# An attention stage re-ordered: feature maps stationary in kv, slot logits from transposed x, three engines in source order

## The chip, the cores and the metric

One core of a Trainium2 chip runs the whole program. The metric is the device time of one execution in microseconds. The core has five engines with a queue each: TensorE (matmuls, PE in the profile), VectorE (DVE), ScalarE (ACT), GpSimd (POOL) and SyncE (SP), which here issues the transfers. PEld is TensorE loading its stationary operand.

## What is computed

Linear attention over 4 batches, 8 heads, 576 positions and 64 channels with 128 features, followed by two mixtures of experts. The change touches the attention and the slot logits of the first mixture.

```python
def phi(x):
    proj = einsum('bhsd,df->bhsf', x, w_phi)
    proj = proj - max(abs(proj), axis=-1)
    return concatenate([exp(proj), exp(-proj)], axis=-1)
q_p, k_p = phi(q), phi(k)
kv = einsum('bhsf,bhsd->bhfd', k_p, v)
z = sum(k_p, axis=2)
num = einsum('bhsf,bhfd->bhsd', q_p, kv)
den = einsum('bhsf,bhf->bhs', q_p, z) + 1e-06
x = num / den                       # then (2304, 512), heads side by side
logits = x @ moe_phi                # (2304, 32), first mixture
d = softmax(logits, axis=0); c = softmax(logits, axis=1)
slot_input = d.T @ x                # 32 slots, 8 experts, then c @ slot_out
...                                 # second mixture: 8 experts over all tokens
```

## The kernel before

The 2304 tokens are cut into 18 tiles of 128 tokens (NT = 18), all batches in one row. A batch has 4.5 tiles, so tiles 4 and 13 hold two batches, and there are 20 (tile, batch) blocks of v, whose rows of the other batch are zero. All of the attention runs in one loop over i from 0 to 25. The key side works at tile i, the query side at t = i - LAG with LAG = 7, so that iterations 0 to 6 have keys alone, 7 to 17 keys and queries, 18 to 25 queries alone.

- `project` (pk for keys, pq for queries) multiplies a tile of 512 x 128 by the feature matrix into two PSUM banks (heads of even and odd number), and VectorE then takes the largest magnitude per head (mk, mq) and subtracts it (uk, uq). uq and uk have two buffers each, one for each half of a tile.
- `k_exp` makes phik = exp(u), exp(-u) with four ScalarE instructions.
- `kv_acc` accumulates kv transposed, v as the stationary operand and 256 feature columns moving, for a (tile, batch) block. `z_acc` adds phik into zs elementwise on GpSimd, in the key-only part half of it on VectorE.
- `kv_finish`, once per batch, sums zs over partitions with ones (zp), turns kv back through a matrix bd which holds the identity and, beside it, the slot matrix phi (kvp), spreads z (zc), and leaves kvs with XW = 64 + 32 + 1 columns per head: values, slot logits, denominator.
- `q_transpose` turns uq (ut) and takes both exponentials (phiq). `q_num` multiplies phiq by kvs (num), adds 1e-6 to the denominator column, inverts it (rd), scales the 32 logit columns (lgh), sums them over heads (lg), and scales the values (x).
- `slot_inputs` is a generator per group of four tiles (the fifth group has two): column maximum (gm, gmt, mx, dg, gmb), exponential (dd), sums (pcs) and slot inputs (psi), with a running rescaling. `si_step` runs its next part, once in the middle and once at the end of an iteration. `slot_norm` makes the row softmax. `keep_busy` issues transposes that nobody reads.

The kernel uses PSUM as eight banks of 512 columns: the kv accumulator takes two, and a pool of six rotates among all other tiles (`mm`). Up to the end of the loop a planner orders the instructions of each engine; a wrapper `InOrder` makes an engine keep the source's order, and it is put on all five only behind the loop. The weights of the first mixture are 32 units of 1 MB. Their first buffers are free from the start, some become free with the key buffers (`wk`), and four (`wq`) with the query buffers after the loop. Lines written behind the loop stand in the profile under one helper line, L50.

Of the kernel before, what the change touches and what calls it, by code (L numbers as in the profile page):

```python
# [22 lines left out]
XW = D + NS + 1  # L23
# [30 lines left out]
def tile_kernel(ctx: ExitStack, tc: tile.TileContext, a):  # L54
# [84 lines left out]
    zs_t = {}  # L139
# [13 lines left out]
    def kv_acc(t, b):  # L153
        phik = phik_t[t]
        v = vt_t.pop(VBLOCKS.index((t, b)))
        first = b * S // 128 == t
        last = ((b + 1) * S - 1) // 128 == t
        if first:
            kvacc[b] = pacc.tile([128, 1024], F32, tag="kv", name=f"kvacc{b}")
        acc = kvacc[b]  # L160
        for p in range(4):
            for j in range(2):
                PE.matmul(  # L163
                    acc[64 * j:64 * j + 64, p * 256:(p + 1) * 256],
                    v[:, (2 * p + j) * D:(2 * p + j + 1) * D],
                    phik[:, 2 * p + j].rearrange("p c f -> p (c f)"),
                    start=first and p % 2 == 0, stop=last, skip_group_check=True,
                )

    def z_acc(t, b):  # L170
        flat = phik_t[t].rearrange("p h c f -> p (h c f)")
        _, r0, r1 = next(x for x in parts_of(t) if x[0] == b)
        if b not in zs_t:
            z = zs_t[b] = kp.tile([128, 2048], F32, tag="zs", name=f"zs{b}", bufs=1)
            if r0:
                G.memset(z[0:r0], 0.0)
            A.copy(out=z[r0:r1], in_=flat[r0:r1])
        else:
            z = zs_t[b]
            cut = 1024 if t < LAG else 2048  # L180
            G.tensor_tensor(out=z[r0:r1, 0:cut], in0=z[r0:r1, 0:cut], in1=flat[r0:r1, 0:cut], op=ALU.add)  # L181
            if cut < 2048:
                V.tensor_tensor(out=z[r0:r1, cut:], in0=z[r0:r1, cut:], in1=flat[r0:r1, cut:], op=ALU.add)

    def kv_finish(b):

        acc = kvacc.pop(b)
        kvt = kp.tile([128, 1024], F32, tag="kvt", name=f"kvt{b}", bufs=1)
        for i in range(2):
            A.copy(out=kvt[:, i * 512:(i + 1) * 512], in_=acc[:, i * 512:(i + 1) * 512])  # L190
        yield
        zs = zs_t.pop(b)
        zp = mm(f"zp{b}")
        for g in range(4):
            PE.matmul(zp[32 * g:32 * g + 32, :], ones[:, 0:32], zs[:, g * 512:(g + 1) * 512], start=True, stop=True)
        zrow = kp.tile([128, 512], F32, tag="zrow", name=f"zrow{b}", bufs=1)
        V.tensor_copy(out=zrow, in_=zp)
        kvs = qp.tile([128, 2, H, XW], F32, tag=f"kvs{b % 2}", name=f"kvs{b}", bufs=1)
        for c in range(2):
            pss = [mm(f"kvp{b}_{c}_{j}") for j in range(2)]  # L200
            for p in range(4):
                for j in range(2):
                    r = slice(j * D, (j + 1) * D)
                    for g in range(2):
                        f = p * 256 + c * 128 + g * 64
                        PE.matmul(
                            pss[j][g * 64:(g + 1) * 64, p * 96:(p + 1) * 96],
                            kvt[r, f:f + 64], bd[r, p, j * 96:(j + 1) * 96], start=True, stop=True,
                        )
            for j in range(2):  # L210
                (A.copy if j == 0 else V.tensor_copy)(
                    out=kvs[:, c, j::2, 0:XW - 1], in_=pss[j][:, 0:384].rearrange("p (h w) -> p h w", h=4),
                )
        zc = mm(f"zc{b}")
        for j in range(2):
            for c in range(2):
                o = (j * 2 + c) * 4
                for g in range(2):
                    f = j * 256 + c * 128 + g * 64
                    PE.matmul(zc[g * 64:(g + 1) * 64, o:o + 4], zrow[:, f:f + 64], sel_e, start=True, stop=True)  # L220

        for c in range(2):
            V.tensor_copy(
                out=kvs[:, c, :, XW - 1].rearrange("p (g j) -> p j g", j=2),
                in_=zc[:, 0:16].rearrange("p (j c g) -> p j c g", j=2, c=2)[:, :, c, :],
            )
        kvs_t[b] = kvs
        yield
# [19 lines left out]
    x_t, lgh_t = {}, {}  # L248

    def q_num(t, hh):  # L250
# [3 lines left out]
        if hh == 0:  # L254
            lgh_t[t] = qp.tile([128, H, NS], F32, tag="lgh", name=f"lgh{t}", bufs=1)
# [770 lines left out]
```

## Time and profile before

| | |
|---|---|
| median of three runs | 1042.41 us (1038.42 to 1042.95) |
| the profiled execution | 1041.55 us, span 1039.4 us |
| granted TensorE clock, mean | 0.993 of full |
| TensorE busy | 1011.1 us, 97% of the span |
| VectorE, ScalarE, GpSimd busy | 723.7, 549.4, 642.0 us |
| attention, to the last numerators | 0 to 198.7 us |
| first expert matmul of the first mixture | 206.41 us |

The span runs from the first to the last instruction; the execution's own time has about 2 us around it. A busy TensorE need not be at its peak, since its matmuls are pipelined: a group's length in the timeline includes the time in which its last matmul drains, and the distance from one group's start to the next says what it costs. From 300 us on the second mixture fills TensorE.

### The profile page before, as it was taken

Reading aid. Unit: us, or ns where it says so; the run is one execution under the profiler, and the core shown is the slowest. Engines: PE = TensorE matmul, PEld = TensorE weight load, DVE = VectorE, ACT = ScalarE, POOL = GpSimd, SP = SyncE. Lnnn points to the kernel's source line nnn. Section 1 sums busy time; section 2 is a strip of 40 time slices with the busy share of each in tenths; the row PEclk is TensorE's granted clock in tenths of the full one; section 3 lists DMA queues with packets and bytes.
Section 4 is the critical chain, followed back from the end, with each engine's and each line's share of the span. In section 5 each row is a group of like instructions: output and inputs, shape, how many; then the busy total and the mean of one; then the engine's idle time right before and its main releaser. Section 6 shows DMA issues by size and latency. Waiting matters only on the chain.

```text
span 1039.4 us, 25962 instructions
## 1 busy us (share of the span) xinstructions
PE 1011.1 (97%) x10673; PEld 934.9 (90%) x10673; DVE 723.7 (70%) x1498; ACT 549.4 (53%) x965; POOL 642.0 (62%) x408
## 2 busy tenths in 40 slices
PE   7998988998999999999999999999999999999998
PEld 4676767745999999999999999999999999999998
DVE  7888778723688676766766766676676766766765
ACT  5664433224566766665556555555655565556442
POOL 3543510047477858785787778677858785787543
PEclk9998989999999999999999999999999999999999
DMA  8962226398000310040013003100310040000111
GB/s 301 373 210 64 61 76 252 139 417 330 29 1 1 123 42 2 1 163 2 1 42 123 2 1 109 55 2 2 122 43 1 2 163 1 2 2 21 62 42 61
DMA packets 22581, 89.43 MB, mean 86 GB/s; under 512 B 2752, under 2 KB 5568, under 8 KB 14272
## 3 DMA queue, kind: packets, MB, share of 16 engines
q1 hardware_dynamic: 22176, 87.26, 23.1%
q8 instruction: 84, 1.38, 0.5%
q0 software_dynamic: 288, 0.52, 0.2%
q14 instruction: 33, 0.27, 0.1%
HBM read 83.05 MB, written 4.72 MB: 84 GB/s over the span
## 4 chain that ended last, share of the span: by engine, by line
PE 89%; DVE 6%; DMA 2%; issue 1%; POOL 1%; ACT 0%; SPq 0%; DVEq 0%; ACTq 0%; POOLq 0%
PE x L50 38%; PE y L50 19%; PE z L50 16%; PE num L262 4%; PE kvacc L163 2%; PE ut L236 2%; DMA moe_w<-in_moe_w 2%; PE pq L125 1%; PE ps L50 1%; DVE mq L132 1%; PE pk L125 1%; PE ph L50 1%; DVE uq L134 1%; PE po L50 1%; PE pr L50 1%
## 5 line engine op out<-in xcount | busy, mean ns | idle before, releaser
L50 POOL TENSOR_TENSOR hl_s<-s,hh_s 128x512 fp32r<-128x512 f32 x287 | 366.5, 1298 | 213.2 <-ACT hh_s L50 194.0
L50 PE MATMUL x<-w_t,hh_s 128*128 128x256 f32 x1152 | 204.3, 277 | 0.0
L50 ACT ACTIVATE hh_s<-s 128x512 fp32r<-128x512 f32 x288 | 175.5, 629 | 52.2 <-DVE s L50 47.9
L50 ACT ACTIVATE r<-z 128x512 f32<-128x512 f32 x144 | 86.2, 598 | 166.5 <-PE z L50 166.5
L50 PEld LDWEIGHTS x<-w_t,hh_s 128*128 128x128 f32 x1152 | 173.6, 188 | 0.0
L50 DVE SCALAR_TENSOR_TENSOR xo<-x,P,xo 128x256 f32<-128x256 f32 x252 | 120.8, 480 | 71.5 <-PE x L50 71.5
L50 ACT ACTIVATE hh_a<-z 128x512 fp32r<-128x512 f32 x216 | 122.2, 600 | 76.2 <-DVE s L50 75.3
L50 DVE SCALAR_TENSOR_TENSOR s<-z,r 128x512 f32<-128x512 f32 x144 | 98.8, 686 | 87.7 <-ACT hh_a L50 82.6
L50 PE MATMUL x<-w_t,hl_s 128*128 128x256 f32 x576 | 159.5, 277 | 0.0
L50 DVE SCALAR_TENSOR_TENSOR hl_a<-z,hh_a 128x512 fp32r<-128x512 f32 x216 | 147.1, 681 | 0.0
L50 PEld LDWEIGHTS x<-w_t,hl_s 128*128 128x128 f32 x576 | 108.3, 188 | 0.0
L50 PE MATMUL y<-w_t,hh_s 128*128 128x256 f32 x576 | 102.9, 278 | 0.0
L50 PE MATMUL z<-w_b,hh_a 128*128 128x256 f32 x576 | 102.3, 278 | 0.0
L50 PE MATMUL x<-w_t,hh_a 128*128 128x256 f32 x576 | 101.6, 276 | 0.0
L50 PE MATMUL y<-w_b,hh_s 128*128 128x256 f32 x576 | 101.5, 276 | 0.0
L50 PE MATMUL x<-w_b,hh_a 128*128 128x256 f32 x576 | 101.2, 276 | 0.1
L50 DVE SCALAR_TENSOR_TENSOR s<-z,s 128x512 f32<-128x512 f32 x144 | 98.4, 684 | 4.0 <-POOL hl_s L50 1.7
L181 POOL TENSOR_TENSOR zs<-zs,phik 128x2048 f32<-128x2048 f32 (+3 forms) x16 | 60.6, 3786 | 58.0 <-ACT phik L150 55.2
L50 PEld LDWEIGHTS z<-w_b,hh_a 128*128 128x128 f32 x576 | 86.6, 188 | 2.9 <-issue 2.9
L50 PEld LDWEIGHTS y<-w_t,hh_s 128*128 128x128 f32 x576 | 87.4, 188 | 0.0
L50 PEld LDWEIGHTS x<-w_b,hh_a 128*128 128x128 f32 x576 | 86.5, 188 | 0.4 <-ACT hh_a L50 0.4
L50 PEld LDWEIGHTS y<-w_b,hh_s 128*128 128x128 f32 x576 | 86.7, 188 | 0.0
(199 smaller groups left out, 2106.3 us busy)
## 6 DMA issues: line engine op xcount, KB each, us to landing
moe_w<-in_moe_w SPq DMA_DIRECT2D x64, 1024.0 KB, 7.6
vt<-in_vb SPq DMA_DIRECT2D x20, 256.0 KB, 3.8
kt<-in_kT SPq DMA_DIRECT2D x18, 256.0 KB, 5.7
qt<-in_qT SPq DMA_DIRECT2D x18, 256.0 KB, 3.5
out<-xo SPq DMA_DIRECT2D x18, 128.0 KB, 1.7
out<-xo SPq DMA_DIRECT2D x9, 256.0 KB, 2.0
rep<-in_rep POOLq DMA_DIRECT2D x2, 256.0 KB, 9.8
bd<-in_bd SPq DMA_DIRECT2D x1, 384.0 KB, 4.7
```

Source lines behind the costliest of these rows:

```text
L50: return lambda *args, **kwargs: self.tc.keep_in_program_order(make(*args, **kwargs))
L125: PE.matmul(pss[j][g * 64:(g + 1) * 64, p * F:(p + 1) * F], x[r, p * 128 + g * 64:p * 128 + (g + 1) * 64], wbd[r, j * F:(j + 1) * F], star ...
L132: V.tensor_reduce(out=m, in_=h4(pss[j]), axis=AX.X, op=ALU.max, apply_absolute_value=True)
L134: V.tensor_tensor(out=h4(u), in0=h4(pss[j]), in1=m.unsqueeze(2).to_broadcast([128, 4, F]), op=ALU.subtract)
L163: PE.matmul(acc[64 * j:64 * j + 64, p * 256:(p + 1) * 256], v[:, (2 * p + j) * D:(2 * p + j + 1) * D], phik[:, 2 * p + j].rearrange("p c f ...
L181: G.tensor_tensor(out=z[r0:r1, 0:cut], in0=z[r0:r1, 0:cut], in1=flat[r0:r1, 0:cut], op=ALU.add)
L236: PE.transpose(ps[:, j * 128:(j + 1) * 128], uq_t[t][hh][:, j * 128:(j + 1) * 128], ident)
L262: PE.matmul(ps[g * 64:(g + 1) * 64, j * XW:(j + 1) * XW], phiq[:, c, j * 128 + g * 64:j * 128 + (g + 1) * 64], kvs_t[b][:, c, 2 * j + hh, ...
```

## The change

- kv: phik becomes the stationary operand (two halves of 64 features), and v moves, 65 columns per head: a column of ones beside the 64 values makes z in the same matmul. The accumulator takes three banks. z_acc and the matmuls of kv_finish go; three ScalarE copies per batch make kvs, with XW = 65.
- v's tiles are loaded with 65 columns per head, so that each row lands in eight pieces of 256 bytes; GpSimd sets the ones. Six buffers instead of three, each load one iteration earlier.
- Slot logits: x is turned by TensorE (x_turn), copied by ScalarE, and multiplied by phi (x_logits), whose result ScalarE copies into lg. lgh and its sum over heads go.
- PSUM: five banks A to E, each tile's named by hand; the rotation remains for tiles behind the loop.
- TensorE, VectorE and ScalarE keep source order from ahead of the loop. In an iteration with keys the order is now: x_turn(t-1), query projection(t+1), key projection(i+1), both transposes(t), kv block, k_exp, x_logits(t-1), slot step, both numerators(t), a second kv block. Without keys x_turn follows the transposes and x_logits the numerators. The numerators of t come one iteration earlier than before.
- Weights: wa is loaded in iterations 5 to 8 (was 1 to 4), the next seven in 9 to 15 (was 5 to 11); sel4 and wg within the loop. slot_norm is cut in two parts, with its two wide operations on GpSimd for the first three groups; gm4's copy goes to GpSimd.

```diff
-XW = D + NS + 1
+XW = D + 1
+KVB = 6
...
+    def mm(name, bank=None):
+        if bank is None:
+            bank = "ABCDE"[turn_of[0] % 5]
+            turn_of[0] += 1
+        return pmm.tile([128, 512], F32, tag=bank, name=name)
...
+        x = kp.tile([128, H, XW], F32, tag="vt", name=f"vt{i}", bufs=6)
+        SP.dma_start(out=x[:, :, 0:D], in_=a["vb"][i].rearrange("p (h d) -> p h d", h=H))
...
+            G.memset(x[r0:r1, :, D:XW], float(b1 == b))
...
-        pss, us = [mm(f"p{nm}{t}_{j}") for j in range(2)], []
+        pss, us = [mm(f"p{nm}{t}_{j}", ("CD" if nm == "k" else "AB")[j]) for j in range(2)], []
...
+        for m in range(2 * H):
+            j, p, c = m // 8, m // 2 % 4, m % 2
+            h = 2 * p + j
+            o = m // KVB * 512 + m % KVB * XW
+            for g in range(2):
                 PE.matmul(
+                    acc[g * 64:(g + 1) * 64, o:o + XW],
+                    phik[:, h, c, g * 64:(g + 1) * 64], v[:, h, :],
+                    start=first and m % KVB == 0, stop=last, skip_group_check=True,
                 )
...
+        for i in range(3):
+            n = min(KVB, 2 * H - KVB * i) * XW
+            A.copy(out=kvs[:, i * KVB * XW:i * KVB * XW + n], in_=acc[:, i * 512:i * 512 + n])
...
+    def late(t):
+        return "C" if t + LAG + 1 >= NT else "A"
...
-        ps = mm(f"ut{t}_{hh}")
+        ps = mm(f"ut{t}_{hh}", "E" if hh == 0 else late(t))
...
-        ps = mm(f"num{t}_{hh}")
+        ps = mm(f"num{t}_{hh}", "E" if hh == 0 else late(t))
...
+    def x_turn(t):
+        ps = mm(f"xt{t}", "D" if t + LAG + 2 >= NT else "E")
+        for kc in range(KC):
+            PE.transpose(ps[:, kc * 128:(kc + 1) * 128], x_t[t][:, kc * 128:(kc + 1) * 128], ident)
+        xT = qp.tile([128, KC, 128], F32, tag="xT", name=f"xT{t}", bufs=1)
+        A.copy(out=xT.rearrange("p c t -> p (c t)"), in_=ps)
...
+    def x_logits(t):
+        xT = xT_t.pop(t)
+        pl = mm(f"lg{t}", "B")
+        for kc in range(KC):
+            for g in range(2):
+                PE.matmul(pl[g * 64:(g + 1) * 64, 0:NS], xT[:, kc, g * 64:(g + 1) * 64], phi[:, kc, :], start=kc == 0, stop=kc == KC - 1)
+        A.copy(out=lg[:, t, :], in_=pl[:, 0:NS])
...
-        pt = mm(f"gmt{g}")
-        keep_busy(last, 13)
+        pt = mm(f"gmt{g}", "C")
+        keep_busy(last, 5)
...
-        ps, pc = mm(f"psi{g}"), mm(f"pcs{g}")
+        ps, pc = mm(f"psi{g}", "B"), mm(f"pcs{g}", "C")
...
+        W = G if g < 3 else V
...
+    PE, V, A = (InOrder(tc, x) for x in (PE, V, A))
     k_project(0)
     k_exp(0)
     for i in range(NT + LAG + 1):
         t = i - LAG
+        alone = i + 1 >= NT
...
+        if 0 <= t - 1 < NT and not alone:
+            x_turn(t - 1)
+        if 0 <= t + 1 < NT:
+            q_project(t + 1)
         if i + 1 < NT:
             k_project(i + 1)
         if 0 <= t < NT:
             q_transpose(t, 0)
+            q_transpose(t, 1)
+        if 0 <= t - 1 < NT and alone:
+            x_turn(t - 1)
+        bs = [b for b, _, _ in parts_of(i)] if i < NT else []
+        if bs:
+            kv_acc(i, bs[0])
+            if ((bs[0] + 1) * S - 1) // 128 == i:
+                kv_finish(bs[0])
         if i + 1 < NT:
             k_exp(i + 1)
+        if 0 <= t - 1 < NT and not alone:
+            x_logits(t - 1)
+        si_step()
         if 0 <= t < NT:
+            q_num(t, 0)
+            q_num(t, 1)
+        for b in bs[1:]:
+            kv_acc(i, b)
...
```

## Rows read from the trace of the kernel before

**Rows 1.** Windows, core 0; per engine busy us (instructions), then clock, DMA share, GB/s.
```profile
61.19:85.00 23.81, 23.81 (x457) 19.33 (x456) 21.05 (x51) 12.73 (x24) 12.77 (x3) 1.00 0.42 126
...
206.41:245.00 38.59, 36.55 (x425) 15.21 (x426) 7.72 (x41) 10.02 (x20) 20.19 (x14) 1.00 1.02 417
```

**Rows 2.** Timeline of TensorE, a both-sided iteration: start, duration, line, operation, count.
```profile
71.20 1.10 PE L125 MATMUL pq<-wbd,qt 64*64 64x128 f32 x32
72.23 1.95 PE L163 MATMUL kvacc<-phik,vt 128*64 128x256 f32 x16
74.01 1.50 PE L262 MATMUL num<-kvs,phiq 128*64 128x97 f32 x32
75.44 1.10 PE L125 MATMUL pk<-wbd,kt 64*64 64x128 f32 x32
76.48 0.65 PE L236 MATMUL ut<-ident,uq 128*128 128x128 f32 x4
77.06 1.55 PE L262 MATMUL num<-kvs,phiq 128*64 128x97 f32 x32
...
72.23 1.49 PEld L163 LDWEIGHTS kvacc<-phik,vt 128*64 128x64 f32 x16 [0.17 <-issue]
```

**Rows 3.** Timeline of VectorE in the same iteration.
```profile
75.56 0.16 DVE L271 TENSOR_SCALAR rd<-num 128x4 f32<-128x4 f32 x1 [0.67 <-PE num L262]
75.76 0.18 DVE L272 RECIPROCAL rd<-rd 128x4 f32<-128x4 f32 x1
...
76.18 0.42 DVE L281 TENSOR_TENSOR x<-num,rd 128x256 f32<-128x256 f32 x1
...
77.03 1.27 DVE L132 TENSOR_REDUCE mk<-pk 128x4 f32<-128x512 f32 x2
78.23 1.27 DVE L134 TENSOR_TENSOR uk<-pk,mk 128x512 f32<-128x512 f32 x2
```

**Rows 4.** Timeline of ScalarE there; in brackets the idle time before and its releaser.
```profile
77.23 1.09 ACT L239 ACTIVATE phiq<-ut 128x512 f32<-128x512 f32 x2 [3.07 <-PE ut L236]
78.99 2.19 ACT L150 ACTIVATE phik<-uk 128x512 f32<-128x512 f32 x4 [0.68 <-DVE uk L134]
```

**Rows 5.** Timeline, around two summaries of slot logits.
```profile
90.18 4.50 POOL L181 TENSOR_TENSOR zs<-zs,phik 64x2048 f32<-64x2048 f32 x1 [4.30 <-ACT phik L150]
...
91.92 2.80 DVE L318 TENSOR_SCALAR dg<-ident,mx 32x32 f32<-32x32 f32 x1
...
94.87 0.60 PE L327 MATMUL gmb<-dg,ones 32*128 32x32 f32 x2 [3.21 <-DVE rd L271]
95.40 1.98 PE L125 MATMUL pk<-wbd,kt 64*64 64x128 f32 x32
...
139.23 0.60 PE L327 MATMUL gmb<-dg,ones 32*128 32x32 f32 x2 [3.49 <-DVE rd L271]
```

**Rows 6.** Timeline of TensorE: the summary of batch 2, then a kv block.
```profile
106.77 1.06 PE L195 MATMUL zp<-zs,ones 128*32 128x512 f32 x8
...
109.24 0.64 PE L220 MATMUL zc<-sel_e,zrow 128*64 128x4 f32 x16
109.73 1.93 PE L163 MATMUL kvacc<-phik,vt 128*64 128x256 f32 x16
```

**Rows 7.** Timeline of TensorE, one query-only iteration apart.
```profile
183.99 0.66 PE L236 MATMUL ut<-ident,uq 128*128 128x128 f32 x4 [0.49 <-DVE uq L134]
...
189.73 0.66 PE L236 MATMUL ut<-ident,uq 128*128 128x128 f32 x4 [0.49 <-DVE uq L134]
```

**Rows 8.** Timeline of TensorE, last numerators and last transposed maximum.
```profile
197.14 1.56 PE L262 MATMUL num<-kvs,phiq 128*64 128x97 f32 x32
...
200.72 0.33 PE L50 MATMUL gmt<-ident,gm 128*128 128x128 f32 x1 [0.46 <-DVE gm L50]
```

**Rows 9.** Timeline, the first projection and the first reduction.
```profile
3.85 3.69 PE L125 MATMUL pk<-wbd,kt 64*64 64x128 f32 x64 [3.85 <-DMA wbd<-in_wbd]
...
5.86 1.29 DVE L132 TENSOR_REDUCE mk<-pk 128x4 f32<-128x512 f32 x2 [4.45 <-PE pk L125]
```

More of the change, by code (lines that the diff above doesn't have):

```diff
@@ L108, in load_v @@
     def load_v(i):
-        x = kp.tile([128, 512], F32, tag="vt", name=f"vt{i}", bufs=3)
-        SP.dma_start(out=x, in_=a["vb"][i])
+        x = kp.tile([128, H, XW], F32, tag="vt", name=f"vt{i}", bufs=6)
+        SP.dma_start(out=x[:, :, 0:D], in_=a["vb"][i].rearrange("p (h d) -> p h d", h=H))
+        t, b = VBLOCKS[i]
+        parts = parts_of(t)
+        for b1, r0, r1 in parts:
+            G.memset(x[r0:r1, :, D:XW], float(b1 == b))
         vt_t[i] = x
@@ L158, in kv_acc @@
         if first:
-            kvacc[b] = pacc.tile([128, 1024], F32, tag="kv", name=f"kvacc{b}")
+            kvacc[b] = pacc.tile([128, 1536], F32, tag="kv", name=f"kvacc{b}")
         acc = kvacc[b]
-        for p in range(4):
-            for j in range(2):
+        for m in range(2 * H):
[3 more added lines that the diff above has]
+            for g in range(2):
                 PE.matmul(
[L164 to L167, printed above, removed]
-                )
@@ L170, in z_acc @@
[L170 to L183, printed above, removed]
+                    acc[g * 64:(g + 1) * 64, o:o + XW],
@@ L196, in kv_finish @@
[L196 to L226, printed above, removed]
@@ L268, in q_num @@
         pv = ps[:, 0:4 * XW].rearrange("p (h w) -> p h w", h=4)
-        held = hh == 1 and t == NT - 1
-        rd = const.tile([128, 4, 1], F32, name="rd_held") if held else qp.tile([128, 4, 1], F32, tag="rd", name=f"rd{t}_{hh}", bufs=2)
+        rd = qp.tile([128, 4, 1], F32, tag="rd", name=f"rd{t}_{hh}", bufs=2)
         V.tensor_scalar_add(rd, pv[:, :, XW - 1:XW], 1e-6)
@@ L324, in slot_inputs @@
         yield
-        pm = mm(f"gmb{g}")
+        pm = mm(f"gmb{g}", "C")
         keep_busy(last, 6)
@@ L366, in keep_busy @@
         if last and n:
-            pt = mm(f"busy{nbusy[0]}")
+            pt = mm(f"busy{nbusy[0]}", None if nbusy[0] > 3 else "E")
             nbusy[0] += 1
@@ L395, in tile_kernel @@
     ones = load_const("ones", [128, 128])
-    sel_e = load_const("sel_e", [128, 4], kp)
-    bd = load_const("bd", [128, 4, 192], kp)
-    sel4 = load_const("sel4", [128, 128], first)
-    wg = load_const("wg", [128, KC, E])
+    phi = qp.tile([128, KC, NS], F32, name="phi", bufs=1)
+    for j in range(2):
+        SP.dma_start(out=phi[j * D:(j + 1) * D], in_=a["bd"][j * D:(j + 1) * D, :, j * 96 + D:(j + 1) * 96])
+    sel4 = first.tile([128, 128], F32, name="sel4", bufs=1)
+    wg = const.tile([128, KC, E], F32, name="wg", bufs=1)
     lg = early.tile([128, NT, NS], F32, name="lg")
@@ L422, in tile_kernel @@
         t = i - LAG
-        vs = [n for n, (u, _) in enumerate(VBLOCKS) if u == i + 1]
+        alone = i + 1 >= NT
         if i + 3 < NT:
             load_k(i + 3)
+        for n in [n for n, (u, _) in enumerate(VBLOCKS) if u == i + 2]:
+            load_v(n)
         if 0 <= t + 3 < NT:
             load_q(t + 3)
+        if i == 1:
+            SP.dma_start(out=sel4, in_=a["sel4"])
+            SP.dma_start(out=wg, in_=a["wg"])
+        if i == 6:
+            V.tensor_copy(out=sels, in_=sel4[:, 0:NS])
+        if 5 <= i <= 8:
+            load_units(wa, i - 5, 1)
+        elif 9 <= i <= 15:
+            load_units(early if i == 9 else wb, i - 1, 1)
+        if 0 <= t - 1 < NT and not alone:
+            x_turn(t - 1)
+        if 0 <= t + 1 < NT:
+            q_project(t + 1)
         if i + 1 < NT:
@@ L477, in tile_kernel @@
             load_units(wk, 15 + 2 * (i - NT), 2 if i < NT + 3 else 1)
-    PE, V, A, G, SP = (InOrder(tc, x) for x in (PE, V, A, G, SP))
+    G, SP = (InOrder(tc, x) for x in (G, SP))
+    const.tile([128, 8], F32, name="pad", bufs=1)
     while si_steps:
```

118 lines of the change are left out of this document (39 added, 79 removed).

## The prediction

> **What bounds the kernel now.** I read the stage table first. While key and query tiles are both in work, TensorE is busy for the whole of three iterations, and after the attention the weight transfers fill the DMA engines (share 1.02) [rows 1]. So the attention is a TensorE stage followed by a weight stage. Those three both-sided iterations are 23.81/3 = 7.94 us each, and the timeline of one has no gap: each piece starts before the last has drained, with 0.17 us for the weight load to get going where the tile shape changes [rows 2]. VectorE does its part of an iteration inside that time: two reductions and two subtractions each for keys and queries, at 0.60 us spacing, and the small division steps [rows 3]; ScalarE does eight exponentials [rows 4]. [...] Each summary of a batch takes TensorE from 106.77 to 109.73, 2.96 us [rows 6]. With only queries left, an iteration is 189.73 - 183.99 = 5.74 us, 0.49 of it a wait for VectorE [rows 7].
>
> **The change, piece by piece.** All later terms are worked out by following the three queues in source order.
>
> *Matmuls.* A kv block goes from 16 instructions (1.78 us from its start to the next) to 64 of 65 columns; the numerators from 97 to 65 columns, 64 instructions as before; logits add 16 of 32 columns. The price of one 65-column instruction isn't in the trace. From below: kv's 111 ns for 256 columns, scaled, 28; from above: the numerator's unscaled 1.43 us/32 = 45 ns. Sixteen 4-column ones run at (109.73 - 109.24)/16 = 31 ns, and the numerator scaled gives 30 [rows 2, 6]. I take 29 for all 144. Then kv is 1.86 us (was 1.78), numerators 1.86 (was 2 x 1.43 = 2.86), logits 0.46, the transpose of x 0.42 plus a 0.17 shape change. TensorE's own work per iteration thus hardly moves: 7.6 us against 7.94.
>
> [...]
>
> *Waits that source order brings.* Start a both-sided iteration at the transpose of x(t-1), time 0. TensorE: x to 0.42; pq 0.59 to 1.45 (32 in 1.03 - 0.17 = 0.86 [rows 2]); pk to 2.31; first ut 2.48 to 2.90. VectorE starts the q reduction at 0.59 + 1.14 = 1.73 (pq's 1.10 and a semaphore). Its subtraction is next in line, and writes one of two uq buffers, both of which hold tile t until ut has read them: they were filled an iteration ago, and projections now come before transposes. So it starts when the first ut is done, 2.48 + 0.75 (the delay after which ScalarE starts behind a ut [rows 2, 4]) = 3.23, ends 3.91. The second ut shares bank A with pq: 4.06 to 4.48, 1.16 us late. Queued behind it are kv and everything else of TensorE. VectorE's second subtraction starts at 4.81, the four key operations run 5.41 to 8.13 (0.04 between dependent ones, as in the division steps). TensorE: kv 4.65 to 6.51, logits to 6.97, numerators to 7.90 and 8.83. VectorE's division of the second half starts 0.2 later, 9.05, and takes 0.20 + 0.21 + 0.42 = 0.83 [rows 3]; x is there at 9.88 and the next transpose starts at 10.0. TensorE has waited 1.16 + 1.2 us, with nothing that may pass. **10.0 instead of 7.94.**
>
> *Query-only iterations*, from pq = 0: ut 1.03 to 1.87, x to 2.29; ScalarE's four exponentials 1.78 to 3.95 and the x copy to 4.5; numerators 3.02 to 3.95 and 4.1 to 5.03; logits to 5.5; their copy (unseen, 0 to 0.55, the latter a 512-column exponential; I take 0.2) frees bank B at 6.0. **6.0 instead of 5.74.**
>
> *What goes away.* The z additions (VectorE and GpSimd), three of the four 2.96 us summaries inside the dense part, and with GpSimd's long operations the 2.80 us operation and the idles of 3.21 and 3.49 us behind such ones. That GpSimd causes them is read from the overlap alone: its addition runs 90.18 to 94.68, the operation ends at 94.72 [rows 5]. [...]
>
> *Summaries and slots.* ScalarE's three copies per batch (1.3 us, estimated from its 0.55 per 512 columns) run beside TensorE. But in i=13 they precede k_exp(14), and the logits' copy follows that: kv done at 6.7, + 1.3 + 2.2 + 0.2 = 10.4 before bank B is free for psi. TensorE idles from 7.3, 3.1 us, then psi 1.0 and the second kv block: +5.35 for that iteration. The other steps put small VectorE operations, 0.15 to 0.3 us each by the division steps [rows 3], between the key operations and the division, and so delay x: i=12 (maximum, diagonal) +0.55, i=14 (row softmax) +0.6, i=16 (with the rescaling) +0.95. Together **+7.4**. In query-only iterations gmt and pcs go to bank C, which the second ut holds until ScalarE has read it (3.95 instead of 2.29): +1.9 (i=20) and, with psi, +2.2 (i=21).
>
> *Transfers.* v now lands in 256-byte pieces, 8 times as many: unseen; nothing at best. Even 4 us of all 16 engines per load, for three loads in 23.81 us, adds 0.5 to a share of 0.42 [rows 1], still under 1. The loads are issued two tiles ahead, so nothing waits; SP's queue is otherwise emptier, as weights start four iterations later and are first needed after the attention. v's memsets go to a GpSimd that has lost its z.
>
> *Keys alone.* pk now always uses banks C and D, and waits until the subtractions of the tile before are done: 2.72 + 0.15 + 1.14 = 4.0 us from one tile's first reduction to the next's. Tile 0 is at 5.86 as before. The first 64 matmuls took 3.69 us, half speed [rows 9], and now have gaps between them, so I put tile 1 at 10.7 and tile 2, behind a slow kv block, at 15.1; then 19.1, 23.1, 27.1. In i=4 batch 0 ends: kv to 28.9, ScalarE's copies to 30.4, the second kv block, which needs the accumulator, to 32.3, and pk(6) queues behind it: tile 6 at 33.6 (+2.5), tile 7 behind pq(0)'s VectorE work at 39.2. In i=7 pk(8) waits until 41.9, both numerators are done at 48.9, VectorE's key operations at 48.8 and its divisions at 50.4: the first x transpose starts at **50.6**.
>
> *The end.* i=17 has kv (2.46 to 4.3), pcs and psi (to 5.5), numerators (to 7.3), logits and their copy: 8.4 to the next pq. Four at 6.0 and the two with steps, 7.9 and 8.2, make 40.1. i=24 has no projection, its numerators end at 5.2, gmb at 6.75; then x(17) is transposed (7.35), copied behind dd's exponential (8.3), its logits wait in bank B until VectorE has read psi (10.0), and run to 10.65; copy, maximum and the last gmt follow at 11.65, less 0.5 as i=24 needn't wait for bank B: 11.2.
>
> *Sum.* 50.6 + 9 x 10.0 + 7.4 + 8.4 + 40.1 + 11.2 = 207.7 where the last gmt now starts at 200.72 [rows 8]: **+7.0 us**. What follows gmt is unchanged. The profiled execution took 1041.55 (span 1039.4), so 1048.5; the median of the runs, 1042.41, is 0.9 above that execution.
>
> **Rivals.**
> *A, the weights set the end (about the same).* The weight stream is saturated from 206 on [rows 1], and its first loads need query buffers, free after the last numerators: now 197.14 + 1.56 = 198.7, then 201.5, since x and logits follow. If that start decides, +2.8: 1044.3. Against it: later loads need buffers that expert matmuls free, which shift by 7.
> *B, the buffers don't bind (about the same).* If the q subtractions aren't held, bank A is free at 3.28, the second ut waits 0.4 and the pace is 9.2: 9 x 0.8 = 7 back, 1041.5.
> *C, TensorE runs dense (faster).* If neither x nor bank A holds it, because queued work covers them, the pace is TensorE's own: 10.0 - 2.4 = 7.6, and in query-only iterations 0.86 + 1.26 + 1.86 + 0.46 and 0.5 of shape changes, 5.0. Nine and six of them give back 21.6 + 6.0: 1021. It decides once a both-sided iteration is under 9.2. For it: VectorE has less to do; against it: nothing stands between the last numerators and x.
> *D, worse.* The 3.1 us idle drops the clock, as 3.21 did [rows 5] (+3), or 65 columns cost 34 ns or more: 144 x 5 ns x 9 = +6.5. 1055 to 1058.
>
> **How the numbers follow.** Forecast 0.43 (its own range 1044 to 1054), A 0.17, B 0.10, C 0.18, D 0.12. A measurement here tells about 0.5%, 5.2 us, from no change. Slower: the forecast but for 0.08 of its lower edge, and D, 0.47; same: A, B and that edge, 0.35; faster: C, 0.18. The range leaves out most of C and the end of D: 1034 to 1058.
>
> **What would show it.** Right: x transposes 10 us apart with idle ahead of them put down to the x division and of the second ut to uq, no 2.8 us operation on VectorE, psi of i=13 late on bank B, the last gmt near 208. Wrong: both-sided iterations under 9.2 us, or 65-column matmuls far from 29 ns, or a weight stage that is shorter by what the attention lost.

## The result, and the profile after

The changed kernel takes 1056.07 us in the median of its runs (1052.66 to 1059.54) and the kernel before 1041.6 (1038.42 to 1042.95): a ratio of 1.0144, 95% interval 1.0102 to 1.0185. It is slower, by 14.5 us where 7.0 were forecast. The profiled execution took 1055.78 us, its span is 1054.0 us, 14.6 more than before.

All operations of the attention now have the line of the helper that records them, L51; tiles are told apart by name. First two of the engines in a both-sided iteration, TensorE and then VectorE, on the timeline of the changed kernel (in brackets the idle time ahead of a row and what ended it):

```profile
73.83 0.63 PE L51 MATMUL xt<-ident,x 128*128 128x128 f32 x4 [1.01 <-DVE x L51]
74.39 1.10 PE L51 MATMUL pq<-wbd,qt 64*64 64x128 f32 x32
75.31 1.05 PE L51 MATMUL pk<-wbd,kt 64*64 64x128 f32 x32
76.30 0.66 PE L51 MATMUL ut<-ident,uq 128*128 128x128 f32 x4
77.73 0.66 PE L51 MATMUL ut<-ident,uq 128*128 128x128 f32 x4 [0.78 <-DVE uq L51]
78.32 2.09 PE L51 MATMUL kvacc<-vt,phik 128*64 128x65 f32 x64
80.24 0.61 PE L51 MATMUL lg<-phi,xT 128*64 128x32 f32 x16
80.68 2.06 PE L51 MATMUL num<-kvs,phiq 128*64 128x65 f32 x64
83.77 0.63 PE L51 MATMUL xt<-ident,x 128*128 128x128 f32 x4 [1.03 <-DVE x L51]
```

```profile
75.53 0.69 DVE L51 TENSOR_REDUCE mq<-pq 128x4 f32<-128x512 f32 x1 [1.84 <-PE pq L51]
76.99 0.69 DVE L51 TENSOR_TENSOR uq<-pq,mq 128x512 f32<-128x512 f32 x1 [0.77 <-PE ut L51]
77.60 0.68 DVE L51 TENSOR_REDUCE mq<-pq 128x4 f32<-128x512 f32 x1
78.43 0.69 DVE L51 TENSOR_TENSOR uq<-pq,mq 128x512 f32<-128x512 f32 x1 [0.15 <-PE ut L51]
...
83.20 0.42 DVE L51 TENSOR_TENSOR x<-num,rd 128x256 f32<-128x256 f32 x1
```

Where TensorE had no gap [rows 2], it now waits twice in each iteration. The subtraction of VectorE at 76.99 has waited 0.77 us for ut to read a buffer, and so the second ut waits 0.78; the transpose of x waits 1.01 us for VectorE's division, and the next one 1.03 for the division that ends at 83.62. That next transpose starts at 83.77, 9.94 us after this one. kv takes 80.24 - 78.32 = 1.92 us for 64 matmuls (30 ns each), the logits 0.44 for 16 (27.5), against a forecast of 29. VectorE's 2.80 us operation [rows 5] is gone: its like takes 0.23 us at 177.51.

The first transpose of x and what stands ahead of it on TensorE:

```profile
38.71 0.65 PE L51 MATMUL pk<-wbd,kt 64*64 64x128 f32 x12 [0.91 <-issue]
...
44.25 0.66 PE L51 MATMUL pk<-wbd,kt 64*64 64x128 f32 x14 [0.75 <-issue]
...
51.93 0.92 PE L51 MATMUL num<-kvs,phiq 128*64 128x65 f32 x24 [1.81 <-issue]
53.86 0.63 PE L51 MATMUL xt<-ident,x 128*128 128x128 f32 x4 [1.02 <-DVE x L51]
```

Three times TensorE stops in the middle of a group of equal matmuls and waits for nothing that the profile shows, 3.5 us in sum. i=13, where the sums over the slots (psi) share bank B with the logits:

```profile
114.01 1.93 PE L51 MATMUL psi<-x,dd 128*32 128x512 f32 x8 [2.79 <-ACT lg L51]
115.87 2.58 PE L51 MATMUL num<-kvs,phiq 128*64 128x65 f32 x64
```

After 2.79 us of idle time psi takes 1.93 us for eight, where 1.04 is usual, and the numerators 2.58 instead of 2.06; the granted clock is 0.50 from 115 to 117 us. The end of the attention, and the stage of the expert weights (windows: busy us and instructions of PE, PEld, DVE, ACT and POOL, then clock, DMA share, GB/s):

```profile
209.89 0.33 PE L51 MATMUL gmt<-ident,gm 128*128 128x128 f32 x1
```

```profile
63.80:93.70 29.90, 24.48 (x660) 21.92 (x661) 20.36 (x43) 15.38 (x30) 0.34 (x3) 1.00 0.69 239
215.57:259.92 44.35, 39.55 (x437) 16.98 (x438) 8.15 (x42) 11.10 (x22) 20.36 (x14) 0.96 0.98 398
```

Three iterations take 29.90 us instead of 23.81 [rows 1], with TensorE busy for 24.48 of them. The last gmt starts at 209.89 instead of 200.72 [rows 8]. The weight stage, from the first matmul on expert weights to the gate's, lasts 44.35 us, and lasted 246.38 - 206.41 = 39.97 before. Its end, on TensorE, and SP's queue ahead of it:

```profile
247.97 1.07 PE L51 MATMUL ph<-moe_w,sit 128*32 128x256 f32 x16 [3.04 <-DMA moe_w<-in_moe_w]
...
250.36 1.93 PE L51 MATMUL ph<-moe_w,sit 128*32 128x256 f32 x16 [0.95 <-DMA moe_w<-in_moe_w]
252.07 2.62 PE L51 MATMUL po<-moe_w,hz 128*32 128x512 f32 x16
```

```profile
209.32 2.72 SPq L78 DMA_DIRECT2D moe_w<-in_moe_w  x4
```

SP's waits from 150 to 260 us (us in total, times, longest):

```profile
SPq L78 <- PE lg L51: 36.2, 1, 36.2
```

The four weights that take the place of the query buffers are all issued from 209.32 on, after one wait of 36.2 us for the logits; before, the first of them left at 187.84 and the others by 201.5. The stream of weights ends later, and TensorE waits 3.04 us for one. Behind the waits 16 matmuls of ph take 1.93 us instead of 1.07, with a granted clock of 0.79 from 248 to 256 us.

So the 14.6 us of span are: 3.3 more than forecast ahead of the first transpose of x (53.86 against 50.6); a both-sided part of 150.82 - 53.86 = 96.96 us where 9 x 10.0 + 7.4 = 97.4 were forecast; a query part up to the last gmt of 59.1 against 59.7; 4.4 in the weight stage; and 1.1 behind the gate (794.1 us against 793.0). 7.0 + 3.26 - 0.44 - 0.63 + 4.38 + 1.06 = 14.6.

### The profile page after: what moved, and what is told of

Same layout as the page of the kernel before. It is cut to its first block, busy times and chain, and to the rows that moved or that the text cites. A ratio compares the mean times of both kernels' runs of the same rounds, so it can differ in the third digit from the quotient of the medians.

```text
span 1054.0 us, 27856 instructions
## 1 busy us (share of the span) xinstructions
PE 1001.8 (95%) x11633; PEld 945.3 (90%) x11633; DVE 690.9 (66%) x1407; ACT 553.6 (53%) x993; POOL 583.4 (55%) x424
## 3 DMA queue, kind: packets, MB, share of 16 engines
q8 instruction: 92, 1.51, 0.6%
## 4 chain that ended last, share of the span: by engine, by line
PE 91%; DVE 4%; DMA 2%; issue 1%; ACT 1%; SPq 0%; DVEq 0%; ACTq 0%
PE x L51 37%; PE y L51 19%; PE z L51 16%; PE num L51 3%; PE kvacc L51 3%; PE pq L51 2%; PE ut L51 2%; PE pk L51 2%; PE ps L51 1%; DMA moe_w<-in_moe_w 1%; PE po L51 1%; PE ph L51 1%; DVE uq L51 1%; DVE uk L51 1%; DVE mk L51 1%
## 5 line engine op out<-in xcount | busy, mean ns | idle before, releaser
L51 POOL TENSOR_TENSOR hl_s<-s,hh_s 128x512 fp32r<-128x512 f32 x287 | 366.3, 1298 | 214.7 <-ACT hh_s L51 192.3
L51 PE MATMUL x<-w_t,hh_s 128*128 128x256 f32 x1152 | 204.6, 277 | 0.0
L51 ACT ACTIVATE hh_s<-s 128x512 fp32r<-128x512 f32 x288 | 175.8, 630 | 51.8 <-DVE s L51 48.7
L51 ACT ACTIVATE r<-z 128x512 f32<-128x512 f32 x144 | 86.1, 598 | 167.5 <-PE z L51 167.3
L51 PEld LDWEIGHTS x<-w_t,hh_s 128*128 128x128 f32 x1152 | 173.9, 188 | 0.0
L51 DVE SCALAR_TENSOR_TENSOR xo<-x,P,xo 128x256 f32<-128x256 f32 x252 | 120.5, 478 | 71.7 <-PE x L51 71.7
L51 ACT ACTIVATE hh_a<-z 128x512 fp32r<-128x512 f32 x216 | 122.2, 600 | 75.7 <-DVE s L51 74.7
L51 PE MATMUL x<-w_t,hl_s 128*128 128x256 f32 x576 | 159.7, 277 | 0.0
L51 DVE SCALAR_TENSOR_TENSOR s<-z,r 128x512 f32<-128x512 f32 x144 | 98.6, 685 | 88.4 <-ACT hh_a L51 83.1
L51 DVE SCALAR_TENSOR_TENSOR hl_a<-z,hh_a 128x512 fp32r<-128x512 f32 x216 | 146.7, 679 | 0.0
L51 PEld LDWEIGHTS x<-w_t,hl_s 128*128 128x128 f32 x576 | 108.5, 188 | 0.0
L51 PE MATMUL y<-w_t,hh_s 128*128 128x256 f32 x576 | 103.2, 279 | 0.0
L51 PE MATMUL z<-w_b,hh_a 128*128 128x256 f32 x576 | 102.3, 278 | 0.0
L51 PE MATMUL x<-w_t,hh_a 128*128 128x256 f32 x576 | 101.5, 276 | 0.0
L51 PE MATMUL y<-w_b,hh_s 128*128 128x256 f32 x576 | 101.5, 276 | 0.0
L51 PE MATMUL x<-w_b,hh_a 128*128 128x256 f32 x576 | 101.3, 276 | 0.1
L51 DVE SCALAR_TENSOR_TENSOR s<-z,s 128x512 f32<-128x512 f32 x144 | 98.2, 682 | 3.7 <-POOL hl_s L51 1.7
L51 PEld LDWEIGHTS z<-w_b,hh_a 128*128 128x128 f32 x576 | 86.6, 188 | 2.9 <-issue 2.9
L51 PEld LDWEIGHTS y<-w_t,hh_s 128*128 128x128 f32 x576 | 87.7, 188 | 0.0
L51 PEld LDWEIGHTS x<-w_b,hh_a 128*128 128x128 f32 x576 | 86.5, 188 | 0.4 <-ACT hh_a L51 0.4
L51 PEld LDWEIGHTS x<-w_t,hh_a 128*128 128x128 f32 x576 | 86.7, 188 | 0.0
L51 PEld LDWEIGHTS y<-w_b,hh_s 128*128 128x128 f32 x576 | 86.7, 188 | 0.0
```

The costliest lines, as they stand in the source:

```text
L51: return lambda *args, **kwargs: self.tc.keep_in_program_order(make(*args, **kwargs))
```

## Experiments

All times are medians; ratios are to runs of the kernel before on the same chip (1040.5 to 1042.2).

**Source order.**

```
-    PE, V, A = (InOrder(tc, x) for x in (PE, V, A))     # ahead of the loop
...
-    G, SP = (InOrder(tc, x) for x in (G, SP))           # behind it
+    PE, V, A, G, SP = (InOrder(tc, x) for x in (PE, V, A, G, SP))
```

> The changed kernel without source order in the loop: TensorE, VectorE and ScalarE are ordered by the planner as in the kernel before, all else stays. Theory (order makes the waits): transposes move ahead of projections, a both-sided iteration falls to 8.0 to 8.8 us, the last gmt to about 200, the time to 1043 to 1048. Rival (banks named by hand and the chain through x make them, whatever the order): 9.5 us or more per iteration, 1054 or more.

1043.91 us, ratio 1.0032 (1.0019 to 1.0045). Source order is worth 12 of the 14.5 us, but not where the forecast had put it. The gate comes 13.5 us earlier (246.40): the first transpose of x at 49.38 (-4.5, of which 1.7 are shorter idles without a releaser, 1.81 us in sum for 3.47), the both-sided iterations up to i=13 0.8 less in five, i=13 itself 12.83 us instead of 16.22 (-3.4), the query part -3.1, the weight stage 42.44 instead of 44.35 (-1.9). The pace is nearly that of source order: the four iterations from 49.38 to 88.36 take 9.20 to 10.20 us, 9.75 in the mean, where source order has 9.96. TensorE has only short idles of 0.2 to 0.3 us there, with rows such as these in place of two groups of 32:

```profile
89.42 0.33 PE L134 MATMUL pk<-wbd,kt 64*64 64x128 f32 x2
89.52 0.28 PE L134 MATMUL pq<-wbd,qt 64*64 64x128 f32 x2
...
```

From 86.78 to 90.60, less 0.56 for x, the 64 projections take 3.26 us; in source order they took 1.91. Why they are slower when mixed wasn't tried. The attention ends 2.4 us before that of the kernel before (last gmt 198.28 against 200.72), and the longer weight stage takes it back to the tenth.

**The query buffers.**

```
-            u = pool.tile([128, 512], F32, tag=f"u{nm}", name=f"u{nm}{t}_{j}", bufs=2)
+            u = pool.tile([128, 512], F32, tag=f"u{nm}", name=f"u{nm}{t}_{j}", bufs=4 if nm == "q" else 2)
```

> The changed kernel with four uq buffers instead of two, nothing else. Theory (VectorE's q subtraction is held by a uq buffer, and the second ut behind it by bank A): the idle of 0.78 us ahead of the second ut goes to about 0.1, a both-sided iteration falls from 9.95 to about 9.2 us, the last gmt from 209.9 to about 203, the time by 6 to 7 us to some 1049. Rival (TensorE's or VectorE's own work sets the pace, the buffer wait is slack): the iteration stays within 0.2 us of 9.95 and the time within 2 us of 1056.

1051.02 us, ratio 1.0083 (1.006 to 1.0107).

```profile
83.37 0.63 PE L51 MATMUL xt<-ident,x 128*128 128x128 f32 x4 [1.03 <-DVE x L51]
...
85.83 0.66 PE L51 MATMUL ut<-ident,uq 128*128 128x128 f32 x4
86.79 0.66 PE L51 MATMUL ut<-ident,uq 128*128 128x128 f32 x4 [0.30 <-PE ut L51]
87.37 2.09 PE L51 MATMUL kvacc<-vt,phik 128*64 128x65 f32 x64
...
92.82 0.63 PE L51 MATMUL xt<-ident,x 128*128 128x128 f32 x4 [1.03 <-DVE x L51]
```

The wait for uq is gone and an iteration is 9.45 us here; the wait for x stays. The last gmt comes 6.4 us earlier (203.46), the gate 6.2. That the buffers hold the second ut is shown. Of the 6.2 us the profiled execution kept 3.5 (the medians differ by 5.1): behind the gate it took 796.8 us instead of 794.1. No part of the edit explains that, and this stretch takes 793.6 to 796.9 us in the profiles of the changed kernel and its twelve variants.

**Bank B.**

```
+        if 0 <= t - 1 < NT and not alone:
+            x_logits(t - 1)
         if i + 1 < NT:
             k_exp(i + 1)
-        if 0 <= t - 1 < NT and not alone:
-            x_logits(t - 1)
```

> The logits of a tile stand ahead of the exponentials of the next keys in source order. Theory that bank B's wait in i=13 is a matter of ScalarE's queue: the 2.79 us idle of TensorE ahead of psi goes, the last gmt comes 2.5 to 3 us earlier (207 instead of 209.89), the other both-sided iterations stay at 9.9 to 10.0 us, and the total is 1053.3. Rival: the logits' copy now stands in ScalarE's queue until the kv block is done, the exponentials of the keys come later by up to 2 us, and the next kv block waits for them: iterations of 10.5 or more, total 1058 or more.

1053.46 us, ratio 1.011 (1.0091 to 1.0129).

```profile
114.08 1.07 PE L51 MATMUL psi<-x,dd 128*32 128x512 f32 x8 [0.73 <-ACT lg L51]
115.08 2.09 PE L51 MATMUL num<-kvs,phiq 128*64 128x65 f32 x64
```

The 2.79 us are 0.73, i=13 takes 12.79 us instead of 16.22, and the slow matmuls behind the idle are gone too. Other iterations stay at 9.94, so the rival (keys late) falls. Last gmt 206.77.

**phi.**

```
-    phi = qp.tile([128, KC, NS], F32, name="phi", bufs=1)
+    phi = first.tile([128, KC, NS], F32, name="phi", bufs=1)
```

> The changed kernel with the slot matrix phi kept outside the query buffers, nothing else. Theory (the four weight loads behind the loop wait for the last logits, because the first of them takes phi's place and the others queue behind it): the first of the four is issued some 15 us earlier, near 195, the last gmt stays at 209.9, the time from the first ph to pgate falls from 44.4 to 40 to 42 us, and the 3 us wait for weights at 248 with the slow clock behind it goes: some 1052. Rival (the weight stage is longer since expert matmuls free buffers later, or since one PSUM bank is missing): that stage stays at 44 us.

1053.59 us, ratio 1.0115 (1.0074 to 1.0156). The first of the four weights is issued at 195.20 instead of 209.32; the last gmt stays (210.12), and the weight stage is 256.65 - 215.80 = 40.85 us, 3.5 of the 4.4 back:

```profile
245.61 1.07 PE L51 MATMUL ph<-moe_w,sit 128*32 128x256 f32 x16 [0.45 <-DMA moe_w<-in_moe_w]
...
248.01 1.07 PE L51 MATMUL ph<-moe_w,sit 128*32 128x256 f32 x16 [0.96 <-DMA moe_w<-in_moe_w]
248.90 1.90 PE L51 MATMUL po<-moe_w,hz 128*32 128x512 f32 x16
```

A 512-byte row of one constant, read by the last logits, had held a 1 MB weight. It had held only that one: the other three are issued from 209.59 on here too, after waits of 10.0 us for x and 4.0 for the logits, so that the 3.5 us come from a single load that starts 14.1 us earlier.

**The three repairs together**, still in source order.

> Source order kept, with the three single repairs together: four buffers for the shifted queries, logits ahead of the exponentials of the next keys, phi outside the query buffers. If the terms add: 6.4 (buffers, at the last gmt) + 2.8 (bank B) + 3.3 (weight stage) = 12.5 less at the gate, which is 1043.5 in total and level with the kernel before. If they overlap, because a shorter attention only meets a weight stream that can't start earlier: 1047 to 1050.

1041.51 us, ratio 1.0 (0.9987 to 1.0014): the whole loss is gone. The last gmt is at 199.99, the gate at 245.25, the weight stage 39.59 us. The gate comes 14.7 us earlier where the three terms were added to 12.5. The attention gives 9.9 for the 9.2 of its two terms, and the weight stage 4.8 for 3.3, with all four weights issued by 195.8; why these are more wasn't tried.

```profile
82.91 0.63 PE L51 MATMUL xt<-ident,x 128*128 128x128 f32 x4 [1.03 <-DVE x L51]
...
85.38 1.42 PE L51 MATMUL ut<-ident,uq 128*128 128x128 f32 x8
...
92.18 0.63 PE L51 MATMUL xt<-ident,x 128*128 128x128 f32 x4 [1.03 <-DVE x L51]
```

An iteration is 9.27 us; what is left is the wait for x.

**phi without source order.** The edits of the first and the fourth run together.

> The run without source order reached the last maximum's transpose 2.4 us earlier than the kernel before (198.28 against 200.72) and lost exactly that in the weight stage (42.44 us against 39.97), so it ended level. In it the first weight tile of the four that take the query buffers' place is still held until the last logits have read phi. Theory that this one tile sets the weight stage: with phi outside the query buffers the weight stage returns to 40 to 40.9 us (it was 40.85 with phi moved in source order), the gate follows at 244.5 to 245, and the total is 1042 to 1042.5 against 1043.9. Rival, the later tiles (transposed x is also read by the last logits) keep the stream late when the attention is shorter: 42.4 as before, 1043.9.

1041.61 us, ratio 1.0006 (0.9992 to 1.002), 2.3 less than without source order alone. The weight stage is 248.05 - 207.94 = 40.11 us, as the theory had it. The attention of this execution ended 4 us later (202.26): it has 1.73 us of idle that nothing ends at 61.44, and an iteration of 11.64 us around it.

**The idles that nothing ends.** The next six runs are about the 3.5 us ahead of the first transpose of x.

The first four weights four iterations later, the next seven one later:

```
-        if 5 <= i <= 8:
-            load_units(wa, i - 5, 1)
-        elif 9 <= i <= 15:
-            load_units(early if i == 9 else wb, i - 1, 1)
+        if 9 <= i <= 12:
+            load_units(wa, i - 9, 1)
+        if 10 <= i <= 16:
+            load_units(early if i == 10 else wb, i - 2, 1)
```

> The changed kernel with the first eleven weight loads four and one iterations later (9 to 12 and 10 to 16 instead of 5 to 8 and 9 to 15). Theory (TensorE's idles without a releaser at 38.7, 44.2 and 51.9, together 3.5 us, are instruction fetches queued behind weights and 256-byte pieces on full DMA engines): the idles go, the first x transpose moves from 53.9 to 50.4 to 51, the last gmt to about 206.5, the time to about 1052.5. Rival 1 (they come from the number of instructions alone): the first x transpose stays at 53.9. Rival 2 (they only move with the weights): as long ones appear in the iterations from 9 on.

1057.66 us, ratio 1.0154 (1.0138 to 1.0171). It told nothing: SP has no source order in the loop, and the first weight was issued at 29.15 us instead of 26.15.

v in whole rows:

```
-        SP.dma_start(out=x[:, :, 0:D], in_=a["vb"][i].rearrange("p (h d) -> p h d", h=H))
+        y = kp.tile([128, DM], F32, tag="vd", name=f"vd{i}", bufs=2)
+        SP.dma_start(out=y, in_=a["vb"][i])
+        G.tensor_copy(out=x[:, :, 0:D], in_=y.rearrange("p (h d) -> p h d", h=H))
```

> v is loaded in whole rows of 2 KB into a tile of its own, and GpSimd copies it into the 65-column tile; all else as in the changed kernel. Theory that the 256-byte pieces are what makes the transfers late ahead of the first transpose of x (idles of TensorE of 0.91, 0.75 and 1.81 us that no engine ends, with the transfer engines full): these idles go, the first transpose of x comes at 50.4 to 51.5 instead of 53.86, and the total falls by 2.5 to 3.5, to 1053. Rival, the idles come with the full transfer engines whatever the size of the pieces, because two expert weights of 1 MB are under way then: first transpose within 1 us of 53.86, total 1055 to 1057. A second rival: the GpSimd copy makes v late for the second kv block, and the total rises.

1056.88 us, ratio 1.014 (1.0125 to 1.0156).

```profile
39.40 0.65 PE L51 MATMUL pk<-wbd,kt 64*64 64x128 f32 x11 [1.71 <-issue]
...
51.59 0.92 PE L51 MATMUL num<-kvs,phiq 128*64 128x65 f32 x23 [2.31 <-issue]
53.52 1.09 PE L51 MATMUL xt<-ident,x 128*128 128x128 f32 x4 [1.01 <-DVE x L51]
```

The pieces are gone and the idles are not, 4.0 us of them; the first transpose is at 53.52. So the idles don't need the small pieces. What the pieces add to them isn't separated: the first weight also left earlier, at 17.59 us instead of 26.15, and the share from 20 to 54 us stayed at 0.96.

Weights from i=12 on, in place of the four lines taken out above, in three forms: the changed kernel, with the three repairs, and without source order (there with phi moved and four buffers for the shifted queries).

```
+        if 12 <= i <= 13:
+            load_units(wa, 2 * (i - 12), 2)
+        elif i == 14:
+            load_units(early, 8, 1)
+            load_units(wb, 9, 1)
+        elif 15 <= i <= 17:
+            load_units(wb, 10 + 2 * (i - 15), 2 if i < 17 else 1)
```

> The run meant to bring the expert weights later didn't: SP runs ahead of TensorE, and the first of them was issued at 29.15 us instead of 26.15. Here the first eleven weights are issued from i=12 to 17, after 70 us by SP's waits for key buffers; all else as in the changed kernel. Theory: TensorE's idles that no engine ends come where its next block of instructions is late because the transfer engines are full. [...] Then without weights the 0.91, 0.75 and 1.81 us go, the first transpose of x comes at 50.4 to 51, and the total is 1052.5 to 1053.5. Rival: v, keys and queries alone are enough to make the blocks late, or the idles have nothing to do with transfers: first transpose at 53 to 54, total 1056. What could undo the gain: weights that land too late for the stage after the attention, shown by a wait for weights at its start.

> The three repairs in source order together with the later weights. In the run with the three repairs idles of 2.39 and 0.77 us that no engine ends stood between 57 and 70 us. If they come from the weights, 3 us go: 1038.5 against 1041.5, and the last gmt near 197. If the idles only move to where the weights now load, 1041 to 1042.

> Without source order, phi outside the query buffers, four buffers for the shifted queries, and the later weights. The run with phi moved had idles of 0.58, 0.77, 0.51, 0.51 and 1.73 us that no engine ends before 62 us, 4.1 in all. If the weights cause them: the last gmt at 198 or earlier and the total 1037.5 to 1038.5, the first version below both kernels. If not: 1041 to 1042.

1057.06 us (ratio 1.0139, 1.0106 to 1.0171), 1041.45 (1.0005, 0.9991 to 1.0018) and 1044.08 (1.002, 1.0 to 1.004). None is a test: SP issued the first weight at 30.05, 30.23 and 30.77 us all the same, and the idles stayed, 2.36 us ahead of the first transpose in the first, 3.85 and 0.72 in the second, 2.61 at 61.71 in the third. They gave something else. Summing the counts of TensorE's rows from the start, the longer idles that nothing ends stand after the same numbers of matmuls in every version, to within two. (The one exception, 1.54 us at 7.44 in the run with phi moved, is put down to VectorE's uk in the changed kernel.)

The repairs and the weights from i=12 on once more, with SP in source order as well:

```
-    PE, V, A = (InOrder(tc, x) for x in (PE, V, A))
+    PE, V, A, SP = (InOrder(tc, x) for x in (PE, V, A, SP))
```

> The later weights of the last three runs weren't later: SP's queue is in no source order, and the first weight was issued at 30 us in each. Here SP too keeps source order in the loop, on top of the three repairs, with the weights from i=12 on; SP then reaches them only behind the key tile whose buffer the projection of i=10 frees, at 75 us or later. In all twelve profiles of changed kernels TensorE's longer idles that no engine ends, ahead of 80 us, stand at the same places of its stream: after 724, 850, 976, 1102, 1229, 1354 or 1480 matmuls, 126 apart or a multiple of it, however the work is ordered. Theory: a block of instructions ends there and the next is late when the transfer engines are full of weights. Then no idle of over 0.5 us stands at these places ahead of 75 us, the first transpose of x comes at 49.5 or earlier, the last gmt at 196 to 197 instead of 199.99, and the total is 1038 to 1039. Rival: keys, queries and v alone make the blocks late, and idles of 2 us or more in sum stay ahead of 75 us: 1041.5. A third way: the weights now load later, the idles come after 75 us, and as much is lost there: 1041.5, with the first transpose early.

1043.3 us, ratio 1.0017 (1.0005 to 1.0029). The first weight is issued at 74.34 us, and the transfer engines' share from 20 to 54 us falls to 0.56. The windows of that stretch, in the order kernel before, changed kernel, three repairs, this run:

```profile
20.00:54.00 34.00, 31.13 (x494) 20.12 (x496) 30.65 (x47) 21.11 (x38) 20.38 (x8) 1.00 0.98 370
20.00:54.00 34.00, 26.23 (x742) 23.24 (x738) 22.16 (x39) 16.89 (x31) 0.88 (x8) 1.00 0.96 311
20.00:54.00 34.00, 29.07 (x800) 25.55 (x795) 23.94 (x42) 18.27 (x35) 0.88 (x8) 1.00 1.01 323
20.00:54.00 34.00, 29.01 (x792) 26.11 (x788) 23.21 (x41) 17.38 (x32) 0.89 (x8) 0.96 0.56 142
```

TensorE in this run:

```profile
48.23 0.92 PE L51 MATMUL num<-kvs,phiq 128*64 128x65 f32 x24 [0.55 <-issue]
50.18 0.63 PE L51 MATMUL xt<-ident,x 128*128 128x128 f32 x4 [1.03 <-DVE x L51]
...
95.11 1.27 PE L51 MATMUL kvacc<-vt,phik 128*64 128x65 f32 x36 [0.74 <-issue]
...
101.77 1.43 PE L51 MATMUL pq<-wbd,qt 64*64 64x128 f32 x27 [0.67 <-issue]
...
124.64 0.45 PE L51 MATMUL num<-kvs,phiq 128*64 128x65 f32 x7 [1.94 <-issue]
```

The third way of the expectation: ahead of 75 us one idle of 0.55 us is left, and the first transpose of x comes at 50.18, where the forecast had 50.6. The last gmt is at 204.26, where 196 to 197 was expected. The idles follow the weights: 0.74, 0.67 and 1.94 us once these are under way, after 1984, 2109 and 2616 matmuls, which again are 126 or a multiple of it, to within three, away from the others. Nothing is won, since SP's weights only meet another part of a stream that is just as dense.

One execution of each version was profiled. In the changed kernel and its first eleven variants, all with weights from 17 to 31 us on, the idles of 0.4 us or more make 1.8 to 6.0 us ahead of 75 us, and from 75 to 135 us there is only one, of 0.88; in this run they make 0.55 and 3.35. That these idles go with the weights' transfers is shown by that. Full transfer engines aren't enough, though: the kernel before, with 494 matmuls in the 34 us instead of 742, has no such idle at a share of 0.98, and the run with the three repairs has none ahead of 57 us at 1.01.

That it is TensorE's own instructions that come late is argued from the places. The transfers that the profile names instruction (queue q8) move 1.51 MB in 92 packets in the changed kernel, 16.4 KB each. The profile counts 11633 matmuls and as many weight loads there, 253 instructions for each packet; in the kernel before it counts 10673 of each and 84 packets, 254 for each. The places, 126 matmuls and their 126 weight loads apart, are 252. The profile doesn't say whose instructions a packet holds, and no run here moved these packets alone: that TensorE waits for one is the author's estimate from these counts, and isn't shown.

## Why the prediction was right, and why it was too small

The direction and the mechanism of the both-sided iterations hold. The size doesn't: 1056.07 us lies outside the forecast's own range of 1044 to 1054, and the wider range holds it by the price of rival D, whose mechanism gave about 1 us here. That part is luck. What was missing are two terms put at nothing, the transfers ahead of the first x and the weight stage. Each point by its own step:

*Waits that source order brings.* 9.94 us an iteration for 10.0, with both waits at their places: 0.78 us for uq (1.16 forecast, of which a part is the matmuls' own time) and 1.0 for x (1.2). The runs with four buffers show that the first is the buffers' and bank A's, and give the 9.2 of rival B: 9.27 with all repairs. Only the name was too wide: without source order the pace is hardly better, 9.75, with mixed projections, for which the forecast had no term.

*Matmuls.* 30 ns and 27.5 for the 29 taken.

*Summaries and slots.* i=13's wait 2.79 for 3.1, and it is ScalarE's queue that makes it (logits first: 0.73). i=12, 13, 14 and 16 cost 10.33, 16.22, 10.32 and 10.31 us, 7.2 in all above 10.0 each, for 7.4. i=13 was forecast at 15.35: its wait is 0.3 shorter, and rival D's clock, 0.50 behind the idle as from 95 to 98 us in the kernel before, makes psi and the numerators 1.4 us longer.

*Query-only iterations, the end.* 59.1 us for 59.7; one iteration, from the transpose of x at 161.97 to the next at 167.91, is 5.94 for 6.0, and the two with steps are 7.54 and 7.86 for 7.9 and 8.2. The wait for bank C is there in the first of these, though the profile names no releaser for it:

```profile
174.42 2.06 ACT L51 ACTIVATE phiq<-ut 128x512 f32<-128x512 f32 x4 [1.77 <-PE ut L51]
176.58 0.30 PE L51 MATMUL gmt<-ident,gm 128*128 128x128 f32 x1 [1.33 <-issue]
```

ScalarE's last read of bank C ends at 176.48, and gmt starts 0.10 later; the gmt at 202.04 idles 1.13 us and starts 0.11 after such a read. The share of the transfer engines is 0.00 around both. So "issue" alone doesn't tell one kind of idle from another.

*Transfers, keys alone.* "So nothing waits" failed, by 3.3 us. It was read from the share of 0.42 from 61 to 85 us [rows 1], where the kernel before has 0.98 from 20 to 54. v's pieces lie within the 0 to 4 us a load that were allowed, by an estimate: at the bytes of the kernel before, 7.78 share points per MB from 20 to 54 us, the 10.48 MB of the changed kernel would take 81.5 points and took 94.5; 13.0% of 34 us is 4.4 us for seven loads, 0.63 each. What the step left out, by the estimate above, is TensorE's own stream of instructions, with 64 instructions for a kv block where 16 had been, beside weights that already filled the engines. With the weights away the first transpose came at 50.18; but with the three repairs and the weights in their place it came at 49.83, in an execution whose idles stand at 57.07 and 69.90. So the 3.3 us are the idles, and where they fall in an execution stays open.

*"What follows gmt is unchanged."* This is the step that failed most: 4.4 us in the weight stage. Rival A had its mechanism, the loads that need the query buffers, and made it an alternative to the forecast instead of a term of it. The text saw that logits now read these buffers last, but dated the loads by numerators plus 2.8 us, where phi, in the first of the four places, holds that place's load, and SP's queue behind it, until 209.32. Moving phi let this one load go at 195.20 and brought back 3.5 of the 4.4. The 1.1 us behind the gate (794.1 against 793.0) can't be put down to the change: its variants take 793.6 to 796.9 there.

*Rival C* (dense TensorE): never near; the division stands between the last numerators and x in each version in source order, 1.0 us, and no both-sided iteration read here is under 9.2.

## What to carry to other kernels

When a schedule is fixed by hand, write down for each buffer who reads it last, then look who is queued behind its next writer: all three repairs here were one buffer count, one line's place and one constant's pool, and together they gave back 14.5 us. A later end of one stage isn't only a shift of the next: ask which of its loads were waiting for the stage's buffers, and add that to the sum instead of keeping it as a rival. Before moving transfers in the source, look at the queue's own timeline: a queue that keeps no source order issues them where its waits let it (with the weights placed from i=12 on, SP issued the first at 30.23 us without source order and at 74.34 with it).

## What the runs showed of the hardware

TensorE's long idles without a releaser stand, ahead of 80 us, after 724, 850, 976, 1102, 1229 or 1354 matmuls in twelve versions that differ in order, buffers and transfers; one of 0.37 us stands after 1480, one of 0.46 after 597. After a long one TensorE is often slower for a while. Behind the idles of 2.20 us (run with four buffers, after 976), 2.31 (v in whole rows), 2.36 and 3.85 (weights from i=12 on, alone and with the three repairs), and behind one of 1.73 (phi without source order), 32 projections take 1.98 or 1.99 us instead of 1.10. Behind 2.39 (three repairs) 37 matmuls of kv take 2.32 us, where 64 take 2.09 otherwise; behind 2.61 (weights from i=12 on, without source order) the four of xt take 1.11 instead of 0.63. In the changed kernel this didn't come behind one of 1.81 after 976: the projections at 54.42 take 1.10, and the granted clock is 1.00 from 50 to 56 us. In the run with four buffers:

```profile
50.00:52.00 2.00, 0.97 (x24) 0.87 (x21) 0.76 (x3) 0.00 (x0) 0.00 (x0) 0.66 1.07 357
52.00:56.00 4.00, 4.00 (x68) 3.63 (x66) 1.28 (x2) 0.59 (x1) 0.00 (x0) 0.50 0.80 286
```

The granted clock is 0.50 from 52 to 56 us, and its projections take 1.98 us for 32 there. How often that happens in an execution differs, and with it the first transpose of x: it came at 49.83 us with the three repairs, and at 54.48 where the source places the weights later too, of which the first was issued at 25.07 and at 30.23.
